# A wait on GpSimd in the attention turns, and the written order of the weight loads behind them, in an attention and spectral feed-forward kernel

## The chip, the cores and the metric

The kernel runs on one core of one Trainium2 chip, as one launch. The metric is device time in microseconds (us). Three runs of the kernel before gave 726.14, 727.07 and 729.10 us; their median is 727.07 us.

## The reference

The inputs are q, k and v of 4 batches, 8 heads, 576 positions and 64 columns, a small network (w1, b1, w2) for a position bias, and two feed-forward weights of float64 numbers. Cut to what matters:

```python
scores = scale * q @ k.T + bias            # bias from relu(x @ w1 + b1) @ w2, x = log distances
attn = exp(scores - max) / (sum + 1e-9)
x = (attn @ v), heads side by side         # (4, 576, 512)
mixed = real(fft(fft(x, axis=1), axis=2))
u = x + mixed
un = (u - mean) / sqrt(var + 1e-06)
out = u + relu(un @ w_ch1) @ w_ch2         # w_ch1 (512, 2048), w_ch2 (2048, 512)
```

## The kernel before, in words

The work has three stages. First the bias is made and the scores of the first unit are begun. Then come the attention turns: a unit is two heads of one batch, there are 16 units, and turn n (`turn_of`, line 552) runs the scores of unit n, the rest of unit n - 1 (transposes, product with v, division) and the preparation of unit n + 1. Turns 1 to 14 are written out as a list of steps (`SECOND`, `ORDER`), the end of the attention as another (`TAIL`). Last come the Fourier products and the feed-forward layers, batch after batch; the first batch is called the first dense batch here (`dense`, called with n_first = 2).

Products are made of float32 numbers split into a high and a low part. In a turn GpSimd makes the splits of unit n + 1 (`prep`, line 203): the steps K1 and K2 for k, L2 and M2 for the second half of q, L1 and M1 for the first half. The M steps are the low parts (line 218), the last of a turn is M1.

The feed-forward weights arrive as float64 words. In ten of the turns (`WIDE`: 2, 3, 5, 6, 7, 9, 10, 11, 13, 14) two blocks are turned into float32, one of the first weight matrix (steps W0 to W3) and one of the second (U0 to U3), by `widen` (line 155). Step 0 is GpSimd's (line 163), steps 1 to 3 are VectorE's (DVE): line 166 clears bits of the raw words, line 167 joins two words, line 168 joins the result to that of step 0. The steps s and t then store a block to memory, f and g load the raw words of the block for the next turn (line 159), y loads v (line 201), k and q load the operands of the unit after next. All these loads and stores go through the queue of SyncE (SP), in the order of the list.

In the turns the order on TensorE (PE), DVE and ScalarE (ACT) is the list's, and from turn 2 on that on GpSimd (POOL) and SP as well. In the list the DVE steps of a turn's second half stand as U1, U2, U3, W1, D8, D7, W2, Y2, Y1, W3, and then D2, D1 of the next turn; a D step adds the bias and takes the row's extreme (line 296), an X step is ACT's exponential (line 311), O copies the product with v out of PSUM (line 501), Y divides into x (lines 526 and 530), P transposes (line 443). z sends two columns of 64 reciprocals across partitions by DMA (`across_halves`, line 514).

Around the first dense batch the order on PE, ACT and GpSimd is still written until `fixed.close()`; that on SP is not, and a scheduler chooses it there. `begin` (the function `first` of `widen_rest`) starts loading the raw words of the six remaining blocks of either matrix, whose widening (`res`) is spread over the batch, with step 0 on ACT (line 161).

Of the kernel before, what the change touches and what calls it, by code (L numbers as in the profile page):

```python
# [9 lines left out]
F32 = mybir.dt.float32  # L10
F32R = mybir.dt.float32r
I32 = mybir.dt.int32
# [8 lines left out]
P = 128  # L21
# [5 lines left out]
L0, L1, L2 = 0, 42, 64  # L27
# [20 lines left out]

ORDER = """
S2 U0 D2 Q0' S1 P0' D1 V0' P2' K1 V2' S4 Q1' S0 K2 D4 D0 P1' S6 L2 M2 P3' D6 S3 V1' P4' V3' W0 V4' S5 R' VR0' D3  # L50
D5 S8 E'' X0 X5 vR1' z' X2 k q U1 U2 S7 A0' X1 U3 W1 D8 L1 X6 D7 A1' A2' X8 X3 W2 t g X4 A3' Y2'' Y1'' A4' O' W3
X7 s y f M1
""".split()

SECOND = """
# [76 lines left out]
def body(ctx, tc, a, out):  # L132
    nc = tc.nc
# [21 lines left out]
    def widen(src, dst, raw, q=nc.sync, on_act=False):  # L155
        words = raw.bitcast(I32).rearrange("p (n t) -> p n t", t=2)
        lo, hi = words[:, :, 0], words[:, :, 1]
        m = dst.bitcast(I32)
        q.dma_start(raw, src)
        if on_act:  # L160
            first = lambda: nc.scalar.activation(dst, hi.bitcast(F32), AF.Copy, scale=2.0 ** -112)
        else:
            first = lambda: nc.gpsimd.tensor_scalar(dst, hi.bitcast(F32), 2.0 ** -112, 0.0, ALU.mult, ALU.add)
        return [
            first,
            lambda: nc.vector.tensor_scalar(hi, hi, -0x80000000, None, ALU.bitwise_and),
            lambda: nc.vector.scalar_tensor_tensor(hi, lo, 29, hi, ALU.logical_shift_right, ALU.bitwise_or),
            lambda: nc.vector.scalar_tensor_tensor(m, m, 3, hi, ALU.logical_shift_left, ALU.bitwise_or),
        ]
# [249 lines left out]
    with ExitStack() as st:  # L419
# [93 lines left out]

        def across_halves(u):
            for h, mine in enumerate(half):
                nc.sync.dma_start(rrs[u][half[1 - h], h:h + 1], rss[u][mine, 8:9])

        def scaled(u, w):
            hp, b = units[u]
# [32 lines left out]
        def turn_of(n, pieces):  # L552

            for i, w in enumerate(SECOND if n == 1 else ORDER):
                w, u = w.rstrip("'"), n - w.count("'")
                if w[0] in "WUstfg":
                    if n >= 2:
                        widened(n, w)
                elif w in PREP:
                    if pieces:  # L560
                        pieces[PREP.index(w)]()
                elif w in "kq":
                    if 2 <= n < U - 2:
                        load(n + 2, [w + "T"])
                elif w == "y":
                    if 1 <= n < U - 1:
                        load_v(n + 1)
                elif 0 <= u < U and (u or n == 1 or w[0] not in "SDX"):
                    steps[w[0]](u, w)
# [7 lines left out]
        wide = {}  # L577

        def raw_tile(rp):
            return rp.tile([P, DM], I64, tag="raw", name="raw")  # L580

        def fetch(which, n):

            f = wide.get("next" + which, 0)
            if f == len(WIDE):
                return
            wide["next" + which] = f + 1
            rp = rawp if which == "W" else rawu
            dst = rp.tile([P, DM], F32, tag="wf", name="wf")
            src, to = (a["m1"][f], w1_d[f].rearrange("p k c -> p (k c)")) if which == "W" else (a["m2"][P * f:P * f + P], w2_d[f])  # L590
            wide[which] = widen(src, dst, raw_tile(rp)) + [lambda: nc.sync.dma_start(to, dst)]

        def widened(n, name):

            if name in "fg":
                if n in WIDE and n + 1 in WIDE:
                    fetch("WU"["fg".index(name)], n + 1)
            elif n in WIDE:
                if name in "st":
                    wide["WU"["st".index(name)]][4]()  # L600
                else:
                    wide[name[0]][int(name[1])]()
# [369 lines left out]
        def dense(ut, tiles, store, n_first=0, mix=None, begin=None):  # L972
# [10 lines left out]
            def w2_load(f):  # L983
                wfs[f] = w2p.tile([P, DM], F32, tag="w2f", name="w2f")
                nc.sync.dma_start(wfs[f], w2_d[f])
# [46 lines left out]
                    store(t)  # L1032

            if n_first:
                for f in range(1, len(WIDE)):
                    w1_load(f)
                    if f < 3:
                        w2_load(f - 1)
                    if f == 3:
                        begin()  # L1040
                w1_load(0)
                part = lambda i: mix.fold(nc.vector, 0, i)
                for step, i in (
                        (w1_parts, 1), (part, 0), (part, 1), (relu_parts, 0), (w2_parts, 0), (part, 2),
                        (mix.fold_hi, 0), (w1_parts, 2), (up, 1), (mix.fold_lo, 0), (relu_parts, 1), (w2_parts, 1),
                        (down, 0)):
                    step(i)
                fixed.close()
            pieces = []
            for f in range(n_first, NF):  # L1050
# [7 lines left out]
        def widen_rest():  # L1058

            token_tile("raw")  # L1060
            raws = [raw_tile(rawp), raw_tile(rawd)] + [
                toks["raw"][:, 1024 * i:1024 * i + 1024].bitcast(I64) for i in range(2)]
            todo = {}

            def start(h):
                f = h // 2
                raw = raws[h % 4]
                if h % 2:
                    dst = (rawp, rawd)[f % 2].tile([P, DM], F32, tag="wf", name="wf")
                    todo[h] = widen(a["m2"][P * f:P * f + P], dst, raw, on_act=True)  # L1070
                    todo[h].append(lambda: nc.sync.dma_start(w2_d[f], dst))
                else:
                    dst = w1[f]
                    todo[h] = widen(a["m1"][f], dst, raw, on_act=True)
                    todo[h].append(lambda: nc.sync.dma_start(w1_d[f].rearrange("p k c -> p (k c)"), dst))

            def first():
                for h in range(2 * len(WIDE), 2 * len(WIDE) + 4):
                    start(h)

            res = []
            for h in range(2 * len(WIDE), 2 * NF):
                early = .1 if h < 2 * len(WIDE) + 2 else 1.
                for c, i in ((.7, 0), (.7, 1), (.8, 2), (.9, 3)):
                    res.append((c * early, lambda h=h, i=i: todo[h][i]()))
                res.append((.05, lambda h=h: todo[h][4]()))
                if h + 4 < 2 * NF:
                    res.append((.05, lambda h=h: start(h + 4)))
            return first, res
# [38 lines left out]
        class Pair:  # L1128
# [119 lines left out]
            def w2_load(self, f, more=False):  # L1248
                rp, tg = (rawd if f % 4 else rawp, "wf") if more and f % 2 == 0 else (w2p, "w2f")
                wf = self.wfs[f] = rp.tile([P, DM], F32, tag=tg, name="w2f")  # L1250
                nc.sync.dma_start(wf, w2_d[f])
# [281 lines left out]
```

## Time and profile before

| | |
|---|---|
| median of three runs | 727.07 us |
| the profiled execution | 727.17 us, of which the span is 725.4 us |
| PE busy | 695.9 us (96%) |
| DVE busy | 477.7 us (66%) |
| ACT busy | 434.6 us (60%) |
| GpSimd busy | 328.6 us (45%) |
| granted clock of PE, mean over the span | 0.993 |

The span is the time from the first to the last instruction of the program. The shares are means over stages with different limits: in the attention turns all four engines are loaded, in the dense batches PE alone is. A time on the left of a row is counted from the span's start. The bracket at a row's end says how long the engine had been idle and what ended it.

### The profile page before, as it was taken

To read this page: it belongs to the slowest core of one execution; us is meant where nothing else is said; L and a number is where in the kernel's file an instruction comes from. 1 tells how busy PE (TensorE), PEld (TensorE's weight loads), DVE (VectorE), ACT (ScalarE), POOL (GpSimd) and SP (SyncE) were. 2 spreads that over 40 slices of the span, in tenths; PEclk is the share of its full clock that TensorE was granted. 3 is DMA by queue.
4 is the path that set the end of the run, shared out by engine and by line. 5 is a ranking of instruction groups with operands and counts; after the bars stand their busy time and mean duration, and the time that the engine had idled before them with its cause. 6 is when DMAs were issued, how large, how long until landed. Compare 5 with 4: busy or idle time off the path is not lost.

```text
span 725.4 us, 15300 instructions
## 1 busy us (share of the span) xinstructions
PE 695.9 (96%) x5787; PEld 559.2 (77%) x5787; DVE 477.7 (66%) x1014; ACT 434.6 (60%) x853; POOL 328.6 (45%) x292
## 2 busy tenths in 40 slices
PE   6999999999999989799999999999999999999997
PEld 3457778778778777588888888878788888888896
DVE  7988697997997977676583766566643434453443
ACT  8998999899989787543433433264434232344453
POOL 0002547447447461344544354568645543444342
PEclk9999999999999999899999999999999999999999
DMA  8887487687687621754421311113222214642432
GB/s 225 213 225 198 155 291 222 182 292 221 195 284 220 229 89 52 275 177 157 147 88 58 102 35 67 35 42 101 100 76 87 73 59 130 212 129 81 131 103 72
DMA packets 49945, 105.72 MB, mean 146 GB/s; under 512 B 8944, under 2 KB 9584, under 8 KB 48752
## 3 DMA queue, kind: packets, MB, share of 16 engines
q1 hardware_dynamic: 49152, 101.09, 45.3%
q0 software_dynamic: 288, 3.08, 1.2%
q8 instruction: 45, 0.74, 0.4%
q10 hardware_dynamic: 432, 0.59, 0.2%
q14 instruction: 28, 0.23, 0.1%
HBM read 81.00 MB, written 21.07 MB: 141 GB/s over the span
## 4 chain that ended last, share of the span: by engine, by line
PE 77%; DMA 6%; ACT 6%; DVE 4%; issue 3%; POOL 2%; SPq 1%; DVEq 0%; POOLq 0%; ACTq 0%
PE hp L998 15%; PE acc L1023 15%; PE acc L1269 12%; PE s L275 6%; PE t L492 6%; PE t L443 4%; PE bps L405 4%; PE hpy L1238 3%; PE hpx L1238 3%; PE hpa L1238 3%; PE zp L705 3%; DMA raw<-m 2%; PE abp L725 2%; ACT p L311 2%; PE hpb L1238 1%
## 5 line engine op out<-in xcount | busy, mean ns | idle before, releaser
L964 POOL TENSOR_TENSOR w2l<-w2f,w2h 128x512 fp32r<-128x512 f32 x64 | 85.2, 1331 | 99.3 <-ACT w2h L963 92.0
L296 DVE CUSTOM_DVE_ANT_0 p<-s,bias 128x576 f32<-128x576 f32 x128 | 93.7, 757 | 27.5 <-PE s L275 23.1
L964 POOL TENSOR_TENSOR w1l<-w,w1h 128x512 fp32r<-128x512 f32 x55 | 72.4, 1317 | 76.5 <-ACT w1h L963 72.5
L311 ACT ACTIVATE p<-p,nm 128x576 f32<-128x576 f32 x128 | 97.7, 765 | 11.9 <-DVE nm L296 11.8
L433 ACT ACTIVATE pt<-t 128x1024 f32<-128x1024 f32 (+2 forms) x97 | 79.1, 868 | 5.5 <-PE t L443 3.4
L492 PE MATMUL t<-pt,v 128*64 128x288 f32 x640 | 81.1, 408 | 0.5 <-ACT pt L433 0.5
L963 ACT ACTIVATE w2h<-w2f 128x512 fp32r<-128x512 f32 x80 | 50.2, 628 | 51.6 <-PE acc L1023 22.2
L1007 DVE SCALAR_TENSOR_TENSOR hl<-hp,hh 128x512 fp32r<-128x512 f32 (+1 forms) x48 | 28.9, 602 | 76.7 <-ACT hh L1006 76.6
L963 ACT ACTIVATE w1h<-w 128x512 fp32r<-128x512 f32 x55 | 34.7, 632 | 65.1 <-PE hp L998 52.3
L492 PEld LDWEIGHTS t<-pt,v 128*64 128x64 f32 x640 | 51.0, 137 | 25.4 <-issue 2.4
L1023 PE MATMUL acc<-w2h,hh 128*128 128x512 f32 x160 | 63.2, 396 | 0.0
L275 PE MATMUL s<-kh,qh 64*128 64x288 f32 (+1 forms) x320 | 59.3, 365 | 3.7 <-DVE nm L296 3.2
L1023 PE MATMUL acc<-w2l,hh 128*128 128x512 f32 x160 | 62.4, 391 | 0.0
L1023 PE MATMUL acc<-w2h,hl 128*128 128x512 f32 x160 | 60.0, 393 | 0.0
L405 PE MATMUL bps<-hd,sm 128*32 128x288 f32 x432 | 50.2, 422 | 8.7 <-DVE hd L385 5.3
L443 PE MATMUL t<-ident,p 64*128 64x64 f32 x1152 | 49.5, 226 | 5.9 <-DVE x L526 2.7
L998 PE MATMUL hp<-uh,w1h 128*128 128x512 f32 x124 | 50.0, 403 | 4.2 <-ACT w1h L963 4.2
L443 PEld LDWEIGHTS t<-ident,p 64*128 64x128 f32 x1152 | 45.7, 141 | 9.5 <-issue 3.9
L214 POOL TENSOR_SCALAR kh<-kT 128x640 fp32r<-128x640 f32 x14 | 10.2, 725 | 90.2 <-PE s L275 74.9
L1269 PE MATMUL acc<-w2h,hh 128*128 128x512 f32 x128 | 50.2, 392 | 0.0
L1269 PE MATMUL acc<-w2h,hl 128*128 128x512 f32 x128 | 50.0, 390 | 0.0
L1269 PE MATMUL acc<-w2l,hh 128*128 128x512 f32 x128 | 49.9, 390 | 0.0
(193 smaller groups left out, 1759.8 us busy)
## 6 DMA issues: line engine op xcount, KB each, us to landing
w2f<-w_d SPq DMA_DIRECT2D x80, 256.0 KB, 2.6
raw<-m SPq DMA_DIRECT2D x32, 512.0 KB, 4.4
w<-w_d SPq DMA_DIRECT2D x43, 256.0 KB, 3.1
qT<-qT SPq DMA_DIRECT2D x32, 288.0 KB, 5.2
bias_d<-ring SPq DMA_DIRECT2D x54, 144.0 KB, 2.6
bias<-bias_d SPq DMA_DIRECT2D x24, 288.0 KB, 4.8
w_d<-wf SPq DMA_DIRECT2D x26, 256.0 KB, 2.5
kT<-kT SPq DMA_DIRECT2D x16, 320.0 KB, 4.9
```

Source lines behind the costliest of these rows:

```text
L275: nc.tensor.matmul(ps[:m, c, :CH], st[e, c0:c0 + m], mv[e, k0:k0 + CH], start=i == 0, stop=i == 2, skip_group_check=True)
L296: nc.vector.tensor_tensor_reduce(p, bank.pop((n, i))[:, :, :CH], bias, -0.125, 3.0e38, ALU.add, ALU.min, nms[n][:, blk:blk + 1])
L311: nc.scalar.activation(p, p, AF.Exp, bias=nms[n][:, blk:blk + 1], scale=-1.0, accum_out=sums[n][:, blk:blk + 1])
L405: nc.tensor.matmul(ps[32 * t4:32 * t4 + 32, c, :CH], w2[:, int(rev)], h[:, c * CH:(c + 1) * CH], start=True, stop=True, tile_position=(0, ...
L433: nc.scalar.activation(dst, src, AF.Copy)
L443: nc.tensor.transpose(tp[:m, e, c0:c0 + 64], src[r], ident[r, r])
L492: nc.tensor.matmul(os_[u][e, c, :CH], vt[u][:, j, e], pts[u][:, 2 * j + h if j < 4 else 8, c * CH:(c + 1) * CH], start=j == 0, stop=j == 4 ...
L963: nc.scalar.activation(h, src, AF.Copy)
L964: eng.tensor_tensor(l, src, h.bitcast(F32), ALU.subtract)
L998: nc.tensor.matmul(ps[:, :N], w[wi][:, P * kb:P * kb + P], ut[ui][:, kb, :N], start=i == 0, stop=i == len(mm) - 1)
L1023: nc.tensor.matmul(acc[t], h[i][:, P * t:P * t + P], w[j], start=f == 0 and k == 0, stop=f == NF - 1 and k == 2)
L1269: nc.tensor.matmul(self.acc[t], h[i][:, P * t:P * t + P], w[j], start=f == 0 and k == 0, stop=f == NF - 1 and k == 2)
```

## The change

The step h is new: a copy of one element by GpSimd that reads the raw words of the first matrix' block after W1 has rewritten them; it stands in the list between L1 and M1, so that M1 (the last step on GpSimd in a turn) comes behind it. M1 had stood at the list's end, and on GpSimd was directly behind L1 there too. The steps y and f change places. For the last unit, `across_halves` issues its two DMAs from ACT's queue instead of SP's. In the first dense batch the order on SP is now written as well: the float32 weight blocks first, in a new order, `begin` behind them. The factor that drew the first two blocks' widening to the front of the batch is gone.

```diff
--- before.py
+++ after.py
@@ -48,8 +48,8 @@
 
 ORDER = """
...
-X7 s y f M1
+D5 S8 E'' X0 X5 vR1' z' X2 k q U1 U2 S7 A0' X1 U3 W1 D8 L1 h M1 X6 D7 A1' A2' X8 X3 W2 t g X4 A3' Y2'' Y1'' A4' O' W3
+X7 s f y
 """.split()
 
 SECOND = """
@@ -513,7 +513,8 @@
 
         def across_halves(u):
             for h, mine in enumerate(half):
-                nc.sync.dma_start(rrs[u][half[1 - h], h:h + 1], rss[u][mine, 8:9])
+                q = nc.scalar if u == U - 1 else nc.sync
+                q.dma_start(rrs[u][half[1 - h], h:h + 1], rss[u][mine, 8:9])
 
         def scaled(u, w):
             hp, b = units[u]
@@ -553,7 +554,7 @@
 
             for i, w in enumerate(SECOND if n == 1 else ORDER):
                 w, u = w.rstrip("'"), n - w.count("'")
-                if w[0] in "WUstfg":
+                if w[0] in "WUstfgh":
                     if n >= 2:
                         widened(n, w)
                 elif w in PREP:
@@ -588,7 +589,10 @@
             rp = rawp if which == "W" else rawu
             dst = rp.tile([P, DM], F32, tag="wf", name="wf")
             src, to = (a["m1"][f], w1_d[f].rearrange("p k c -> p (k c)")) if which == "W" else (a["m2"][P * f:P * f + P], w2_d[f])
-            wide[which] = widen(src, dst, raw_tile(rp)) + [lambda: nc.sync.dma_start(to, dst)]
+            raw = raw_tile(rp)
+            if which == "W":
+                wide["raw"] = raw.bitcast(I32)
+            wide[which] = widen(src, dst, raw) + [lambda: nc.sync.dma_start(to, dst)]
 
         def widened(n, name):
 
@@ -596,7 +600,10 @@
                 if n in WIDE and n + 1 in WIDE:
                     fetch("WU"["fg".index(name)], n + 1)
             elif n in WIDE:
-                if name in "st":
+                if name == "h":
+                    hold = smp.tile([P, 1], F32, tag="hold", name="hold", bufs=1)
+                    nc.gpsimd.tensor_copy(hold[0:1], wide["raw"][0:1, 1:2].bitcast(F32))
+                elif name in "st":
                     wide["WU"["st".index(name)]][4]()
                 else:
                     wide[name[0]][int(name[1])]()
@@ -1032,12 +1039,12 @@
                     store(t)
 
             if n_first:
+                loads = st.enter_context(ExitStack())
+                loads.enter_context(tc.manual_schedule(engines={SP_}))
                 for f in range(1, len(WIDE)):
                     w1_load(f)
-                    if f < 3:
-                        w2_load(f - 1)
-                    if f == 3:
-                        begin()
+                    if f in (1, 4):
+                        w2_load(f // 4)
                 w1_load(0)
                 part = lambda i: mix.fold(nc.vector, 0, i)
                 for step, i in (
@@ -1045,6 +1052,8 @@
                         (mix.fold_hi, 0), (w1_parts, 2), (up, 1), (mix.fold_lo, 0), (relu_parts, 1), (w2_parts, 1),
                         (down, 0)):
                     step(i)
+                begin()
+                loads.close()
                 fixed.close()
             pieces = []
             for f in range(n_first, NF):
@@ -1080,9 +1089,8 @@
 
             res = []
             for h in range(2 * len(WIDE), 2 * NF):
-                early = .1 if h < 2 * len(WIDE) + 2 else 1.
                 for c, i in ((.7, 0), (.7, 1), (.8, 2), (.9, 3)):
-                    res.append((c * early, lambda h=h, i=i: todo[h][i]()))
+                    res.append((c, lambda h=h, i=i: todo[h][i]()))
                 res.append((.05, lambda h=h: todo[h][4]()))
                 if h + 4 < 2 * NF:
                     res.append((.05, lambda h=h: start(h + 4)))
```

GpSimd in turn 13, with the last preparation in the list's order; `hold` is the tile of the new copy, `ql` in the row behind it is M1, and `fs` the Fourier table that is loaded behind turn 13. Before:

```order
97 L218 TENSOR_TENSOR kl<-kT,kh 128x640
98 L214 TENSOR_SCALAR qh<-qT 128x576
99 L218 TENSOR_TENSOR ql<-qT,qh 128x576
100 L163 TENSOR_SCALAR wf<-raw 128x512
101 L214 TENSOR_SCALAR qh<-qT 128x576
102 L218 TENSOR_TENSOR ql<-qT,qh 128x576
103 L617 DMA fs<-fs 128x3840
104 L163 TENSOR_SCALAR wf<-raw 128x512
```

The same place now:

```order
106 L214 TENSOR_SCALAR qh<-qT 128x576
107 L218 TENSOR_TENSOR ql<-qT,qh 128x576
108 L163 TENSOR_SCALAR wf<-raw 128x512
109 L214 TENSOR_SCALAR qh<-qT 128x576
110 L605 COPY hold<-raw 1x1
111 L218 TENSOR_TENSOR ql<-qT,qh 128x576
112 L624 DMA fs<-fs 128x3840
113 L163 TENSOR_SCALAR wf<-raw 128x512
```

The copy stands ahead of M1 and of the table's DMA, and both are behind its wait.

SP between the attention and the first dense batch: `raw` are the words of the remaining blocks, `w_` and `w2f` float32 blocks of the two matrices, `rr` the reciprocals (those of the last unit are the second `rr` row of before). Before:

```order
131 L896 DMA w_5003<-w_d 128x512
132 L516 DMA rr<-rs 64x1 x2
133 L159 DMA raw<-m 128x512
134 L516 DMA rr<-rs 64x1 x2
135 L159 DMA raw<-m 128x512 x2
136 L958 DMA w_5388<-w_d 128x512
137 L985 DMA w2f<-w_d 128x512
138 L958 DMA w_5389<-w_d 128x512
139 L985 DMA w2f<-w_d 128x512
140 L958 DMA w_5389<-w_d 128x512
141 L159 DMA raw<-m 128x512
142 L958 DMA w_5390<-w_d 128x512 x2
```

Now:

```order
131 L903 DMA w_5023<-w_d 128x512
132 L517 DMA rr<-rs 64x1 x2
133 L965 DMA w_5408<-w_d 128x512
134 L992 DMA w2f<-w_d 128x512
135 L965 DMA w_5409<-w_d 128x512 x2
136 L965 DMA w_5410<-w_d 128x512
137 L992 DMA w2f<-w_d 128x512
138 L965 DMA w_5410<-w_d 128x512
139 L965 DMA w_5411<-w_d 128x512 x2
140 L965 DMA w_5412<-w_d 128x512 x2
141 L965 DMA w_5408<-w_d 128x512
142 L159 DMA raw<-m 128x512 x4
```

The first block's load no longer stands behind the last unit's reciprocals and three loads of raw words; the four raw loads come behind all twelve blocks.

ACT at the same place, where `uh` and `w1h` are high parts. Before:

```order
216 L835 ACTIVATE uh<-ut 128x4x128 x4
217 L161 ACTIVATE w_5393<-raw 128x512 x2
218 L161 ACTIVATE wf<-raw 128x512
219 L963 ACTIVATE w1h<-w_5388 128x512
220 L1006 ACTIVATE hh<-hp 128x512
221 L963 ACTIVATE w2h<-w2f 128x512
```

Now:

```order
216 L842 ACTIVATE uh<-ut 128x4x128 x4
217 L517 DMA rr<-rs 64x1 x2
218 L970 ACTIVATE w1h<-w_5408 128x512
219 L1013 ACTIVATE hh<-hp 128x512
220 L970 ACTIVATE w2h<-w2f 128x512
```

The three widening steps ahead of the first `w1h` are gone from there, and two DMAs stand in their place.

## Rows read from the trace of the kernel before

**Rows 1.** Timeline of ACT: the copies at line 501 (start, duration).

```profile
80.67 0.65 ACT L501 ACTIVATE ot<-t 128x576 f32<-128x576 f32 x1 [0.36 <-PE t L492]
...
160.89 0.63 ACT L501 ACTIVATE ot<-t 128x576 f32<-128x576 f32 x1
...
173.40 0.63 ACT L501 ACTIVATE ot<-t 128x576 f32<-128x576 f32 x1
...
240.66 0.63 ACT L501 ACTIVATE ot<-t 128x576 f32<-128x576 f32 x1
...
256.45 0.63 ACT L501 ACTIVATE ot<-t 128x576 f32<-128x576 f32 x1
```

**Rows 2.** Groups of DVE, 88 to 256 us: count | busy us, mean ns | idle before.

```profile
L167 DVE SCALAR_TENSOR_TENSOR raw<-raw 128x512 int32<-128x512 int32 x20 | 17.6, 881 | 0.3
L168 DVE SCALAR_TENSOR_TENSOR wf<-wf,raw 128x512 int32<-128x512 int32 x19 | 16.7, 880 | 0.3
L166 DVE TENSOR_SCALAR raw<-raw 128x512 int32<-128x512 int32 x20 | 13.3, 665 | 0.9 <-POOL wf L163 0.6
```

**Rows 3.** Timelines of DVE and PE around the end of turn 9.

```profile
182.42 0.47 DVE L166 TENSOR_SCALAR raw<-raw 128x512 int32<-128x512 int32 x1
...
184.28 0.69 DVE L167 SCALAR_TENSOR_TENSOR raw<-raw 128x512 int32<-128x512 int32 x1
...
187.07 0.75 DVE L296 CUSTOM_DVE_ANT_0 p<-s,bias 128x576 f32<-128x576 f32 x1
...
188.04 0.30 PE L275 MATMUL s<-kh,qh 64*128 64x288 f32 x2
```

**Rows 4.** Timelines of GpSimd and DVE: the first and the last collision with M1.

```profile
100.87 1.59 POOL L218 TENSOR_TENSOR ql<-qT,qh 128x576 fp32r<-128x576 f32 x1
...
101.24 1.80 DVE L167 SCALAR_TENSOR_TENSOR raw<-raw 128x512 int32<-128x512 int32 x1
...
234.00 1.42 POOL L218 TENSOR_TENSOR ql<-qT,qh 128x576 fp32r<-128x576 f32 x1
...
234.40 1.33 DVE L166 TENSOR_SCALAR raw<-raw 128x512 int32<-128x512 int32 x1
```

**Rows 5.** GpSimd, SP; then a stretch: us, engines' busy times, granted clock, DMA, GB/s.

```profile
235.37 0.73 POOL L617 DMA_DIRECT2D fs<-fs  x1
...
237.59 0.53 SPq L159 DMA_DIRECT2D raw<-m  x1
...
245.67 0.66 POOL L163 TENSOR_SCALAR wf<-raw 128x512 f32<-128x512 f32 x1 [9.56 <-DMA raw<-m]
...
257.90:261.30 3.40, 3.40 (x44) 3.38 (x46) 1.02 (x4) 1.60 (x2) 3.32 (x4) 0.50 0.52 153
```

**Rows 6.** SP, ACT, PE at the dense start; then a stretch there.

```profile
291.76 1.10 SPq L516 DMA_DIRECT2D rr<-rs  x2
...
293.50 0.69 ACT L161 ACTIVATE w<-raw 128x512 f32<-128x512 f32 x1
296.88 0.66 ACT L161 ACTIVATE w<-raw 128x512 f32<-128x512 f32 x1 [2.70 <-DMA raw<-m]
299.56 0.66 ACT L161 ACTIVATE wf<-raw 128x512 f32<-128x512 f32 x1 [2.02 <-DMA raw<-m]
...
300.90 0.80 PE L998 MATMUL hp<-uh,w1h 128*128 128x512 f32 x1 [4.15 <-ACT w1h L963]
...
298.90:305.70 6.80, 4.66 (x10) 3.27 (x11) 4.20 (x4) 3.75 (x7) 4.39 (x3) 0.50 1.03 384
```

**Rows 7.** Timelines of SP (end of turn 5) and GpSimd (turn 6).

```profile
133.85 1.60 SPq L201 DMA_DIRECT2D v<-v  x1
...
140.01 0.70 POOL L163 TENSOR_SCALAR wf<-raw 128x512 f32<-128x512 f32 x1 [1.16 <-DMA raw<-m]
```

**Rows 8.** Landing of the reciprocals' DMAs: 90 to 256 us, then 290 to 300 us.

```profile
DMA to landing us min/median/max: 1.6/5.0/9.5
...
DMA to landing us min/median/max: 1.6/1.7/1.7
```

More of the change, by code (lines that the diff above doesn't have):

```diff
@@ L50 @@
 S2 U0 D2 Q0' S1 P0' D1 V0' P2' K1 V2' S4 Q1' S0 K2 D4 D0 P1' S6 L2 M2 P3' D6 S3 V1' P4' V3' W0 V4' S5 R' VR0' D3
-D5 S8 E'' X0 X5 vR1' z' X2 k q U1 U2 S7 A0' X1 U3 W1 D8 L1 X6 D7 A1' A2' X8 X3 W2 t g X4 A3' Y2'' Y1'' A4' O' W3
-X7 s y f M1
+D5 S8 E'' X0 X5 vR1' z' X2 k q U1 U2 S7 A0' X1 U3 W1 D8 L1 h M1 X6 D7 A1' A2' X8 X3 W2 t g X4 A3' Y2'' Y1'' A4' O' W3
+X7 s f y
 """.split()
```

## The prediction

> **What bounds the kernel now.** I read the busy shares first (the table above), then the chain that ended last, then the timelines of the engines turn by turn. PE is busy for 96% of the span, so time can come only from the few places where it idles, runs at the lower clock, or where a turn is longer than PE's own work. The copy O of line 501 marks the turns: it starts at 80.67 us in turn 1 and at 256.45 in turn 14 [rows 1]. These 13 turns take 175.8 us. Turn 8, which widens nothing, takes 173.40 - 160.89 = 12.51 us; 13 such turns are 162.6. So 13.2 us are lost, nearly all in turns that widen.
>
> The reader is to see why in lines 166 to 168. Their 59 instances sum to 47.6 us [rows 2]. Free ones take 0.47 and 0.69 us [rows 3], so that 20 x 0.47 + 39 x 0.69 = 36.3 are due: 11.3 us too many. The long ones begin while GpSimd is in a split and end about 0.58 us after it: line 167 starts at 101.24, M1 ends at 102.46, line 167 at 103.04 [rows 4]. So DVE waits there until GpSimd's instruction ends. U1, U2, U3 and W1 stand ahead of D8 and D7, whose results ACT needs for the last exponentials ahead of O; a delay there is a delay of the turn. Seven turns (3, 5, 6, 7, 10, 11, 13) have such a collision with M1, of 1.80 - 0.69 = 1.11 us in the first and 1.33 - 0.47 = 0.86 in the last [rows 4]; the seven sum to 7.1.
>
> Two more losses lie behind the turns' row. In turn 14 U0 waits for its raw words until 245.67, 8.1 us after their issue, since the Fourier table is in flight from 235.37 on; that turn takes 256.45 - 240.66 = 15.79 us [rows 1], 3.3 over 12.51, and then PE works from 257.9 to 261.3 at a granted clock of 0.50, the 1.2 GHz level, after idling in pieces [rows 5]. And at the start of the first dense batch PE idles 4.15 us until 300.90, behind ACT, which stood at two widening steps waiting for raw words (2.70 and 2.02 us) with the first high part behind them; the clock is at 0.50 from 298.9 to 305.7 [rows 6].
>
> **The change part by part.** The sum is made against the profiled execution, 727.17 us (span 725.4, 1.8 around it); the median, 727.07, is 0.1 less.
>
> *The hold.* M1 now starts behind W1, so none of U1 to W1 can meet it: 7.1 us go. What comes late next is W2, which stands 184.28 - 182.89 = 1.39 us behind W1's end [rows 3]. M1 takes 1.42 us in the last row of GpSimd there [rows 4], so if it starts h after W1's end, W2 loses about h + 1.42 - 1.39 - 0.11 = h - 0.08 (DVE ends 0.58 after the split instead of 0.69 after its own start, hence the 0.11). This delay is less harmful than the old one, because D8 and D7 are done by then. W2's delay runs through Y, W3, D2 and D1 to the score matmul that needs D1's bank: D1 ends at 187.82 and that matmul starts at 188.04 in turn 9, which has no collision [rows 3]. So 0.2 us are free, and PE loses h - 0.28. The copy is not in the trace. From below it is free and h is 0, and PE loses nothing; from above the copy costs a whole 128x512 step, 0.70 us [rows 7], with some 0.2 for two hand-overs h is 0.9, and PE loses 0.6. I take 0.4, nearer to the small end because the copy moves one element, and 0.12 us in each of ten turns: 1.2 us. Behind the hold on GpSimd stand M1, in turn 13 the table's DMA, and the next turn's U0. U0 waits for its DMA anyway. M1 is needed by the next turn's second score step, some 1.8 us ahead of the 188.04 above, so near 186.2; the new end of M1 is 182.9 + 0.4 + 1.4 = 184.7. That cover of 1.5 us hides M1's move; without it each us too much is one of PE.
>
> The Trainium skill (GPSIMD Engine Reference, Instruction dispatch) says that an instruction's completion does not hold back the next one on GpSimd, since each of its cores goes on by itself. By that rule M1 waits for the hold's semaphore and not for the copy, h is about the two hand-overs, and the 1.2 us are 0; no run here shows it.
>
> *Raw words ahead of v.* At the end of turn 5 the load of v holds SP's queue for 1.60 us, and in turn 6 W0 then waits 1.16 us for its words [rows 7]; W0 and L1 meet U1 and U2 there, for 0.8 us by the same count. Moved ahead, the words come 1.6 us earlier and both steps are through: 0.8 us. In the other turns I count nothing. v itself goes a load later and is used only two turns on.
>
> *Turn 14.* The table's DMA now stands behind the hold and M1, so it starts about 234.4 + 2.3 (U1 to W1 free) + 0.4 + 1.4 = 238.5 instead of 235.4 [rows 5], and the raw words of U0, issued at 237.59 before and 0.9 earlier now, go ahead of it. They need not share the engines with it; I estimate half the 8.1 us, so that U0 starts near 240.8 instead of 245.67. GpSimd then reaches W0 and L1 close to U1, or later if their words share the engines with the table. I leave 1.2 of the 3.3 us and count 2.1. If the table still gets in front, the gain is 0; if all fits, 3.2. The 3.4 us at half clock do 1.7 us of work; with the idle pieces gone I count 1.5.
>
> *The dense start.* The last unit's reciprocals held SP until they went at 291.76 [rows 6], and raw loads followed ahead of the first block's. Now that load waits only for the last product with v (PE, near 291.0). ACT's three widening steps are gone from the front; its two DMAs there take some 0.55 each on SP (1.10 for two), so the first high part starts near 293.5 + 1.1 = 294.6, its low part is done on GpSimd near 296.7, and PE's matmuls before it end at 296.75 (300.90 - 4.15). The idle 4.15 goes. So does the half clock: the 4.66 us that PE works in that stretch [rows 6] are 2.3 at 2.4 GHz, 2.3 us less. Together 6.5. What is late next is the fold of the first Fourier product on DVE, which needs x and so the reciprocals. These are issued 2.4 us later, about 294.2, and landed in 1.7 us on an empty queue, 5.0 in the middle under load [rows 8]. With 1.7 DVE goes on near 296.4, the fold's low part is six steps and, I estimate, 4 to 5 us later, and PE needs it near 300.3 (two dozen matmuls behind 296.75): up to 1.1 us of waiting. With 5.0 it is up to 4.4 and perhaps the half clock again. I take 1.5, nearer to the empty queue since ACT's queue holds nothing else, and count 5.0 (bounds 6.5 and 0).
>
> The Trainium skill (DMA: Bandwidth & Descriptors, Queues, rings and completion order) has each DMA engine go round its queues packet by packet. By it the reciprocals on ACT's queue pass the blocks on SP's, and the 1.5 us would be at most 1.1; if they stood behind the blocks, it would be 4.4. In this trace they shared SP's queue with everything, so it shows only the two ends.
>
> *The later widening* moves ACT and DVE work inside a batch where PE is the bound; its cover is PE's lead, and I count 0 (a rival below takes it away).
>
> Sum: 7.1 - 1.2 + 0.8 + 2.1 + 1.5 + 5.0 = 15.3 us; 727.17 - 15.3 = 711.9 us.
>
> **Rivals.** (a) The collision only changes its place. If the hold wakes late, M1 starts as W2 does, W2 loses the whole of M1 in all ten turns, also in 2 and 9 that have none today: between 0.6 and 1.2 us each. At 0.9 that is 9.0 instead of 1.2: 719.7 us. For it: M1 is longer than the gap to W2. Against it: D8 and D7 cover 1.39 of its 1.42 us.
> (b) The reciprocals land late behind the weight blocks on the same DMA engines: PE waits 4.4 us for the fold and falls to half clock for part of it. The dense start is worth 1.4 instead of 5.0: 715.5 us. For it: the median of 5.0. Against it: a queue of their own.
> (c) The hold does not do what it says: turns are bound by ACT and PE together, and the time DVE wins is spent waiting for scores. Then only the dense start counts: 727.2 - 5.0 = 722.2. For it: turn 8 has little slack either. Against it: turns exceed 12.51 by what their collisions sum to, turn by turn.
> (d) Slower: ACT takes its widening steps in order, and now all raw words are loaded behind twelve blocks. If ACT waits at each for 2.7 us, the longest wait at the dense start [rows 6], and the high part behind it is late for PE, each costs 2.7. Six of the twelve blocks eat the gain up; with eight it is 711.9 + 21.6 = 733.5 us. For it: the same order of things cost 4.15 us before. Against it: by then ACT is a whole layer ahead of PE, some 5 us.
>
> **How the numbers follow.** Forecast 0.56 (its own range 707 to 716), (a) 0.15, (b) 0.13, (c) 0.10, (d) 0.06. The low end takes the hold as free, all of turn 14, no wait for the fold, and 1 us from other steps of GpSimd that no longer meet U1 and U2: 711.9 - 1.2 - 1.3 - 1.5 - 1.0 = 706.9, say 707. The upper end reaches to (a) and into (c): 721. A measurement of this kernel can tell about 0.5%, 3.6 us, from no change. Faster than 723.5: the forecast, (b), nearly all of (a) and half or more of (c), 0.87; within 0.5%: 0.07; slower: 0.06.
>
> **What would show it.** In the profile after: lines 166 to 168 at 0.4 to 0.7 us in U1 to W1, and a W2 of 0.7 to 1.1; M1 starting 0.3 to 0.5 us behind W1's end; O to O near 12.6 us in turns 3, 5, 6, 7 and 13; turn 14's U0 some 5 us earlier against turn 13's M1, and no half clock behind it; at the dense start no PE wait over 1.5 us and the first block's load right behind the last product with v. I am wrong if W2 takes over 1.3 us, if O to O stays at 13.5 us with DVE waiting for PE, or if PE waits in the dense batch for a high part behind a widening step.

## The result, and the profile after

The changed kernel takes 718.09 us (median of 4 runs, 716.2 to 718.73); the kernel before took 727.21 us in the same comparison. The ratio is 0.9862, 95% interval 0.9837 to 0.9887. So 9.1 us were won, where 15.3 were forecast: the direction and the whole range (707 to 721) held; the forecast time, 711.9, did not, and the result lies outside the range that the prediction gave the forecast alone (707 to 716).

Where they came from is read from the copies O, as before [rows 1]. ACT's timeline of the changed kernel, the copies of turns 1, 7, 8, 13, 14 and of the last unit:

```profile
81.23 0.65 ACT L501 ACTIVATE ot<-t 128x576 f32<-128x576 f32 x1 [0.36 <-PE t L492]
...
158.08 0.63 ACT L501 ACTIVATE ot<-t 128x576 f32<-128x576 f32 x1
171.62 0.65 ACT L501 ACTIVATE ot<-t 128x576 f32<-128x576 f32 x1 [0.84 <-PE t L492]
...
235.82 0.63 ACT L501 ACTIVATE ot<-t 128x576 f32<-128x576 f32 x1
250.92 0.63 ACT L501 ACTIVATE ot<-t 128x576 f32<-128x576 f32 x1
...
285.27 0.65 ACT L501 ACTIVATE ot<-t 128x576 f32<-128x576 f32 x1 [1.69 <-PE t L492]
```

| stretch | before, us | after, us | won | forecast |
|---|---|---|---|---|
| to the first O | 80.67 | 81.23 | -0.6 | 0 |
| turns 2 to 13 | 159.99 | 154.59 | 5.4 | 6.7 |
| turn 14 | 15.79 | 15.10 | 0.7 | 2.1 |
| to the last O | 34.54 | 34.35 | 0.2 | 1.5 |
| from the last O on | 434.4 | 431.4 | 3.0 | 5.0 |
| span | 725.4 | 716.7 | 8.7 | 15.3 |

(Before, the last O stands at 290.99; the profiled execution after took 718.73 us.) The turns paid 1.3 us less than forecast, of which turn 8 alone took 1.0 (below). Turn 14 and what follows it paid 0.9 of 3.6, the dense start 3.0 of 5.0.

**The turns.** DVE's groups of lines 166 to 168 in the changed kernel, 88 to 252 us; they answer to [rows 2]:

```profile
L167 DVE SCALAR_TENSOR_TENSOR raw<-raw 128x512 int32<-128x512 int32 x20 | 15.9, 796 | 0.3
L168 DVE SCALAR_TENSOR_TENSOR wf<-wf,raw 128x512 int32<-128x512 int32 x20 | 13.8, 690 | 0.3
L166 DVE TENSOR_SCALAR raw<-raw 128x512 int32<-128x512 int32 x20 | 10.1, 503 | 2.3 <-POOL wf L163 2.0
```

They sum to 39.8 us in 60 instances, where 47.6 in 59 stood before. Line 168 is free in all of its 20. Around the end of turn 9, timelines of DVE and GpSimd, with W1, W2 and then the hold and M1 (compare [rows 3]):

```profile
180.89 0.42 DVE L166 TENSOR_SCALAR raw<-raw 128x512 int32<-128x512 int32 x1
...
182.71 0.78 DVE L167 SCALAR_TENSOR_TENSOR raw<-raw 128x512 int32<-128x512 int32 x1
...
181.38 0.17 POOL L605 COPY hold<-raw 1x1 f32<-1x1 f32 x1 [4.49 <-DVE raw L166]
181.52 1.41 POOL L218 TENSOR_TENSOR ql<-qT,qh 128x576 fp32r<-128x576 f32 x1
```

W1 ends at 181.31, M1 starts at 181.52: h is 0.21 us. W2 takes 0.78 instead of 0.69 us. What is left of collisions is that of W0 and L1 with U1 and U2, where W0's words come late (turn 10, GpSimd and DVE):

```profile
191.18 0.65 POOL L163 TENSOR_SCALAR wf<-raw 128x512 f32<-128x512 f32 x1
191.80 0.87 POOL L214 TENSOR_SCALAR qh<-qT 128x576 fp32r<-128x576 f32 x1
...
192.19 1.03 DVE L167 SCALAR_TENSOR_TENSOR raw<-raw 128x512 int32<-128x512 int32 x1
```

Turns 6, 7, 10 and 11 are 12.9 to 13.1 us for that reason, turns 3, 4, 5, 12 and 13 12.6 to 12.7. Turn 9 is 12.9 without a collision in it; that is not explained.

**Turn 14.** Timelines of DVE, GpSimd and SP in the changed kernel, then a stretch behind the turn (us, the engines' busy times, granted clock, DMA share, GB/s); compare [rows 5]:

```profile
230.36 0.49 DVE L166 TENSOR_SCALAR raw<-raw 128x512 int32<-128x512 int32 x1
...
234.27 0.74 POOL L624 DMA_DIRECT2D fs<-fs  x1
237.35 0.65 POOL L163 TENSOR_SCALAR wf<-raw 128x512 f32<-128x512 f32 x1 [2.35 <-DMA raw<-m]
...
246.21 0.66 POOL L163 TENSOR_SCALAR wf<-raw 128x512 f32<-128x512 f32 x1 [3.71 <-DMA raw<-m]
...
236.72 0.39 SPq L159 DMA_DIRECT2D raw<-m  x1
...
246.91 0.88 DVE L166 TENSOR_SCALAR raw<-raw 128x512 int32<-128x512 int32 x1 [1.98 <-POOL wf L163]
...
251.90:255.40 3.50, 3.04 (x42) 3.03 (x44) 1.57 (x6) 1.64 (x4) 3.50 (x3) 0.51 0.56 173
```

U1 of turn 13 starts at 230.36, and U0 of turn 14 at 237.35, 6.99 us behind it; before it was 245.67 - 234.40 = 11.27 us [rows 4, 5]. But the next raw words, W0's, are issued at 236.72 while the table is in flight, and W0 starts at 246.21. DVE then stands 1.98 us at W1. The wait has gone from one weight's words to the other's, and the half clock behind the turn is still there.

**The dense start.** Timelines of ACT, DVE and PE, then three stretches; compare [rows 6]:

```profile
287.22 0.53 ACTq L517 DMA_DIRECT2D rr<-rs  x1
287.79 0.60 ACTq L517 DMA_DIRECT2D rr<-rs  x1
...
292.82 0.29 DVE L531 TENSOR_TENSOR x<-t,rr 128x128 f32<-128x128 f32 x1 [2.77 <-DMA rr<-rs]
...
295.50 0.63 ACT L699 ACTIVATE gh<-ge 128x512 fp32r<-128x512 f32 x1 [3.27 <-DVE ge L694]
...
296.18 1.31 PE L712 MATMUL zp<-fs,gh 128*128 128x320 f32 x4 [2.19 <-ACT gh L699]
...
288.00:291.00 3.00, 3.00 (x13) 2.48 (x14) 2.05 (x4) 0.63 (x1) 1.30 (x1) 1.00 0.89 271
291.00:293.00 2.00, 2.00 (x11) 1.63 (x10) 0.18 (x1) 1.12 (x2) 0.70 (x1) 1.00 0.03 3
...
295.90:299.70 3.80, 3.52 (x13) 3.52 (x14) 2.16 (x5) 2.69 (x6) 2.31 (x2) 0.56 1.01 332
```

The 4.15 us in front of the first `w1h` are gone. The reciprocals, issued at 287.22 and 287.79, land 5.3 and 4.9 us later, when the five blocks issued from 285.31 on are through (the DMA engines are 0.89 busy until 291 and idle then). DVE waits 2.77 us for them. PE waits 2.19 us for the fold, and runs some 3.5 us at about half clock behind it. Part of the 2.19 us is one more collision: the fold's first step on DVE (`pq`) begins beside a split on GpSimd.

```profile
292.30 1.30 POOL L971 TENSOR_TENSOR w2l<-w2f,w2h 128x512 fp32r<-128x512 f32 x1 [1.80 <-ACT w2h L970]
...
293.03 1.66 DVE L692 TENSOR_TENSOR pq<-x 128x1024 f32<-128x1024 f32 x1
```

In experiment 10, where it begins ahead of that split, `pq` takes 1.22 us, so 0.44 us are the split's. In experiment 3 `pq` begins 0.2 us sooner behind the last O, takes 1.88 us, and PE waits the same 2.19.

### The profile page after: what moved, and what is told of

It reads as the page before. It is cut to its first block, busy times and chain, and to the rows that moved or that the text cites. A ratio compares the mean times of both kernels' runs of the same rounds, so it can differ in the third digit from the quotient of the medians.

```text
span 716.7 us, 15317 instructions
## 1 busy us (share of the span) xinstructions
PE 692.2 (97%) x5787; PEld 559.4 (78%) x5787; DVE 469.6 (66%) x1014; ACT 434.8 (61%) x853; POOL 327.6 (46%) x302
## 4 chain that ended last, share of the span: by engine, by line
PE 87%; ACT 4%; DMA 3%; DVE 2%; issue 1%; POOL 1%; SPq 0%; DVEq 0%; ACTq 0%; POOLq 0%
PE acc L1030 15%; PE hp L1005 15%; PE acc L1277 12%; PE t L492 10%; PE s L275 9%; PE t L443 6%; PE bps L405 5%; PE hpy L1246 3%; PE zp L712 3%; PE hpx L1246 3%; PE hpa L1246 3%; PE abp L732 2%; PE hpb L1246 1%; DMA raw<-m 1%; ACT ring L351 1%
```

## The experiments

Each ran in five rounds beside the kernel before (728.1 to 728.4 us there). The gain of one against the changed kernel is worked out from the two ratios to the kernel before, times 728. Each ratio's interval is 1.6 to 2.0 us to either side in experiments 4 to 11, so such a gain is uncertain by some 2.5 us.

**1. The hold alone,** on the kernel before (`L1 h M1` in the list, M1 away from the end, the step h; nothing else).

> The kernel before with the hold alone: step h and M1 behind it; raw words still behind v, the old dense start. Theory (the hold pays the collisions with M1 back in full and costs next to nothing itself): the copies O of turns 2 to 13 lie 160.0 us apart in sum before and 154.6 after the whole change; I expect 154.8 to 155.6 here, line 166 to 168 free of M1 in U1 to W1, the dense start as before (PE idle near 4 us), so 5 to 6 us in all, near 721.5 us. The turn behind the Fourier table gains under 1 us. Rival c of the prediction (turns are bound elsewhere): O to O stays near 13.3 us on average and the time near 727.

722.38 us, ratio 0.9926 (0.9909 to 0.9942): 5.4 us faster. Turns 2 to 13 take 153.7 us in the profile, 6.3 less than before; lines 166 to 168 sum to 39.7 in 59 instances. The dense start is as before (PE waits 4.19 us). So the hold's part stands by itself, and rival (c) falls. Turn 14 was expected to gain up to 1 us; it got 0.84 us longer (16.63). GpSimd there, with the table, U0 and W0:

```profile
231.68 0.74 POOL L623 DMA_DIRECT2D fs<-fs  x1
234.18 0.67 POOL L163 TENSOR_SCALAR wf<-raw 128x512 f32<-128x512 f32 x1 [1.77 <-DMA raw<-m]
...
245.20 0.65 POOL L163 TENSOR_SCALAR wf<-raw 128x512 f32<-128x512 f32 x1 [5.85 <-DMA raw<-m]
```

The hold by itself already moves the wait from U0's words to W0's.

**2. Raw words ahead of v, alone.**

```diff
-X7 s y f M1
+X7 s f y M1
```

> The kernel before with the steps y and f exchanged, and nothing else: raw words ahead of v. The prediction's term: 0.8 us, from turn 6 alone, 726.3 us. Rival: nothing that can be measured (M1 still collides, and a step W0 that comes earlier only meets other steps), 727.1 plus or minus 1. Where it is worth more, step W0 must wait under 1 us for its words in turns 5, 6 and 10 and lines 166 to 168 must sum to less than 47.6 us.

727.98 us, ratio 1.0002 (0.9987 to 1.0017): nothing. In the profile (span 724.5) turns 5, 6 and 13 are 0.5, 0.75 and 0.8 us shorter, turns 7 and 14 0.55 and 0.8 longer; the three lines sum to 45.9 us in 60 instances. What one turn wins is partly lost in another.

**3. The dense part alone,** on the kernel before (ACT's queue for the last reciprocals, SP's written order, `begin` behind it, no early factor).

> The kernel before with the dense part alone (the last unit's reciprocals from ACT's queue, SP's written order, raw words last, no early factor). From the trace after: the idle time and half clock at the dense start fall from about 7 us to about 4, so 3 us, 724.2 us; PE then waits some 2 us for the fold's high part and is at half clock for 3 to 4 us behind it. The prediction's term was 5.0 (722.2). The reciprocals should land about 5 us after their issue here too, if it is the blocks ahead of them that hold them.

724.92 us, ratio 0.9957 (0.9938 to 0.9977): 3.1 us faster. PE waits 2.19 us for the fold's high part, the reciprocals land after 4.2 and 4.7 us, and what follows the last O takes 431.8 us, near the changed kernel's 431.4. The order on SP, `begin`'s place and the dropped factor were not tried apart from each other. The parts sum to 5.4 + 0 + 3.1 = 8.5 us; the whole change has 8.7 by the spans, 9.1 by the medians and 10.0 by its ratio.

**4. The changed kernel without the hold.**

```diff
-... U3 W1 D8 L1 h M1 X6 D7 ...
+... U3 W1 D8 L1 M1 X6 D7 ...
```

> The changed kernel with the step h taken out and M1 right behind L1 again. If the hold is worth 5.5 to 6.5 us and the parts add, this is 718.1 + 6 = 724 us, with the collisions of M1 back in lines 166 to 168 in seven turns and O to O near 13.5 us there. If the earlier raw words carry part of it, it is nearer to 721.

724.22 us, ratio 0.9949 (0.9929 to 0.9969): 6.3 us slower than with it. Turns 3, 5, 6, 7, 10 and 11 are back at 13.6 to 14.2 us, but turns 2 to 13 together are only 4.3 us longer than in the changed kernel (158.85 us; 5.2 if the changed kernel's unexplained wait of 0.94 us in turn 8, below, is set aside). Another 3.0 us are turn 14, which takes 18.11 us. GpSimd and SP there:

```profile
233.24 0.73 POOL L624 DMA_DIRECT2D fs<-fs  x1
...
236.36 1.35 SPq L159 DMA_DIRECT2D raw<-m  x1
...
247.06 0.66 POOL L163 TENSOR_SCALAR wf<-raw 128x512 f32<-128x512 f32 x1 [13.10 <-DMA raw<-m]
```

Without the hold the table goes 3.1 us ahead of U0's words, with it 1.5 us behind them (234.27 against 232.75). So the totals, 5.4 alone and 6.3 here, agree, but they are made up of different parts: part of the hold's worth in the changed kernel is the later issue of the table.

**5. The Fourier table a turn earlier.**

```diff
-            if n == U - 2:
+            if n == U - 3:
                 fs = tabp.tile(...)
```

> The changed kernel with the Fourier table's DMA issued one turn earlier, ahead of turn 13 instead of ahead of turn 14. Theory (turn 14 stays long because the raw words, this time those of W0, share the DMA engines with the table: they were issued at 236.72 us and W0 could start at 246.21): turn 14 falls from 15.1 to 12.7 us, W0 there waits under 1 us, the idle pieces and the half clock behind it go, 1.5 to 3 us more, so 4 to 5 us in all, near 713.5 us. Rival 1: the table only meets the operands of turn 13, that turn gets longer by what turn 14 loses, 718 us. Rival 2: the half clock behind turn 14 comes from the end of the attention itself, and only 2.4 us are won, 715.7 us.

715.57 us, ratio 0.982 (0.9795 to 0.9845): 3.1 us faster than the changed kernel, less than the theory had and little more than the uncertainty. The profiled execution is the slowest of its five (717.78), its span only 0.7 us below the changed kernel's; so the trace does not show where all of the 3.1 us come from. Turn 14 is 14.36 (0.7 less) and the stretch behind it loses its half clock (1.3 less), but turn 13 is 13.90 (1.2 more): GpSimd waits there for kT, and its later steps meet U1 to U3. Two of its rows, GpSimd and DVE in turn 13:

```profile
225.43 0.73 POOL L214 TENSOR_SCALAR kh<-kT 128x640 fp32r<-128x640 f32 x1 [0.75 <-DMA kT<-kT]
...
231.16 1.08 DVE L167 SCALAR_TENSOR_TENSOR raw<-raw 128x512 int32<-128x512 int32 x1
```

Rival 1 holds in part: the table takes its price wherever something else is being loaded.

**6. The last reciprocals back on SP's queue.**

```diff
-                q = nc.scalar if u == U - 1 else nc.sync
+                q = nc.sync
                 q.dma_start(...)
```

> The changed kernel with the last unit's reciprocals back on SP's queue, ahead of the first block's load; nothing else differs. In the changed kernel they were issued at 287.2 and 287.8 us behind five blocks (1.3 MB) issued from 285.31 on, and landed 5.1 us later; the fold waited 2.77 us for them and PE 2.19 us for the fold. Theory (they land late because the blocks are ahead of them in the DMA engines, whatever the queue): on SP they go at 286.1 with nothing ahead, land by 289, the fold is 3 us earlier and PE's 2.19 us and most of the half clock go; the first block comes 1.9 us later, which costs PE about 1 us at its low part. 1.5 to 3 us faster, 715 to 716.5 us. Rival (a DMA of 64 pieces of 4 bytes takes 5 us by itself there): they land at 291, the fold gains 1 us, the first block loses 1: 718 us.

715.41 us, ratio 0.9831 (0.9806 to 0.9857): 2.3 us faster than from ACT's queue, which the times alone do not show clear of the noise; in the trace what follows the last O is 1.9 us shorter (429.6). The reciprocals go first and land after 1.6 and 1.7 us; PE does not wait for the fold and stays at full clock there. It waits 0.42 and 1.12 us for the first block's parts instead, as expected.

**7. Fewer blocks ahead of the reciprocals,** still on ACT's queue.

```diff
                     w1_load(f)
-                    if f in (1, 4):
-                        w2_load(f // 4)
+                    if f == 1:
+                        w2_load(0)
+                        w2_load(1)
```

> The changed kernel with the second block of the second matrix loaded right behind the first one. Its room is free only when the division with the reciprocals is done, and so the three blocks behind it in SP's order wait too: the reciprocals, still on ACT's queue, have two blocks (0.5 MB) ahead of them instead of five. If the bytes ahead decide, they land in 2.5 to 3.5 us instead of 5.1, the fold is 2 us earlier, PE waits under 0.5 us for it and stays at full clock or nearly: 2 to 3.5 us faster, 715 to 716 us. If ACT's queue is slow by itself they take 5 us as before, and it is 718 us. The order of later work in the first dense batch differs from that of the changed kernel; the dense start is read from the trace.

715.56 us, ratio 0.9835 (0.9813 to 0.9857): 2.0 us faster, within the noise by the times; in the trace what follows the last O is 2.5 us shorter (428.9). In its trace the DMA issues from 285 to 295 us, and a stretch:

```profile
rr<-rs ACTq DMA_DIRECT2D x2, 0.2 KB, 2.7
...
292.00:296.00 4.00, 3.92 (x22) 3.32 (x21) 3.03 (x5) 2.10 (x5) 2.24 (x2) 1.00 0.95 306
```

The reciprocals land after 2.9 and 2.5 us, PE has no wait over 0.4 us at the dense start, and the clock stays at 1.00. With none, two and five blocks ahead (6, 7 and the changed kernel) the reciprocals take 1.7, 2.7 and 5.1 us: on ACT's queue the landing goes with the blocks ahead on SP's, and a queue of their own does not take them past.

**8. The hold fourfold.**

```diff
-                    nc.gpsimd.tensor_copy(hold[0:1], wide["raw"][0:1, 1:2].bitcast(F32))
+                    for _ in range(4):
+                        nc.gpsimd.tensor_copy(hold[0:1], wide["raw"][0:1, 1:2].bitcast(F32))
```

> The changed kernel with the hold's copy made four times. One took 0.17 us, so M1 starts 0.72 instead of 0.21 us behind W1. By the prediction's formula W2 loses 0.5 us more in each of ten turns (0.78 becomes 1.3 us) and PE h - 0.28 = 0.44 us: 4.4 us, 722.5 us. Rival (D8 and D7, done by then, leave room for it, and only W2, Y and D2 move): O to O stays at 12.65 us in the turns without other collisions, 718 to 719 us.

720.7 us, ratio 0.9912 (0.9892 to 0.9932): 3.6 us slower. GpSimd and DVE in turn 9:

```profile
183.44 0.88 POOL L606 COPY hold<-raw 1x1 f32<-1x1 f32 x4 [4.29 <-DVE raw L166]
184.29 1.40 POOL L218 TENSOR_TENSOR ql<-qT,qh 128x576 fp32r<-128x576 f32 x1
...
182.94 0.44 DVE L166 TENSOR_SCALAR raw<-raw 128x512 int32<-128x512 int32 x1
184.77 1.48 DVE L167 SCALAR_TENSOR_TENSOR raw<-raw 128x512 int32<-128x512 int32 x1
```

Four copies took 0.88 and not 0.68 us, so h is 184.29 - 183.38 = 0.91. W2 takes 1.48; the formula gives 0.69 + 0.91 - 0.08 = 1.52. PE's part by the formula is 0.91 - 0.28 = 0.63 in a turn behind one that widens. Turns 3, 4 and 12, which in both kernels have no collision but W2's, got 0.61, 0.67 and 0.70 longer: the formula holds, with its 0.2 us of room. Turns 6, 7, 10 and 11 got only 0.28 to 0.40 longer; there U1 and U2 meet fewer of W0 and L1 than in the changed kernel (none in turns 6 and 10). Turn 5 got 0.27 longer and turn 9 0.26 shorter, which the formula does not explain. Turns 2 to 13 got 3.05 longer in all; the changed kernel's unexplained wait in turn 8 (0.94 us), which is missing here, hides part of the price.

**9. The Fourier table behind the last M1 of turn 14.**

```diff
-            if n == U - 2:
-                fs = tabp.tile(...)
-                nc.gpsimd.dma_start(fs, a["fs"])
             turn_of(n, pr)
+            if n == U - 2:
+                fs = tabp.tile(...)
+                nc.gpsimd.dma_start(fs, a["fs"])
```

> The changed kernel with the Fourier table's DMA issued behind the last M1 of turn 14 instead of ahead of that turn. One turn earlier it only moved the trouble: turn 14 fell by 0.7 us and turn 13 rose by 1.2, since the table then met kT and qT there. Here no raw words and no operands are left to load in turn 14's wake, and the first product with the table is 15 us away. Theory (turn 14's 2.5 us over 12.6 and part of what follows are the price of the table in flight): W0 of turn 14 waits under 1 us, turn 14 is 12.6 to 13.2 us, turn 13 stays at 12.7, PE idles 2 us less behind it; 3 to 4.5 us faster than the changed kernel, 713.5 to 715 us. Rival (the half clock and the idle pieces behind turn 14 belong to the end of the attention): only the 2 us of turn 14, 716 us.

712.78 us, ratio 0.9792 (0.9767 to 0.9816): 5.1 us faster than the changed kernel. GpSimd in turn 14, and two stretches:

```profile
236.72 0.65 POOL L163 TENSOR_SCALAR wf<-raw 128x512 f32<-128x512 f32 x1 [2.90 <-DMA raw<-m]
...
241.83 0.66 POOL L163 TENSOR_SCALAR wf<-raw 128x512 f32<-128x512 f32 x1
...
246.81 0.74 POOL L625 DMA_DIRECT2D fs<-fs  x1
...
246.80:253.00 6.20, 5.39 (x102) 4.58 (x98) 4.96 (x13) 5.33 (x12) 5.45 (x5) 1.00 0.77 259
289.00:296.00 7.00, 4.80 (x24) 3.75 (x24) 5.09 (x8) 3.10 (x6) 3.21 (x3) 1.00 0.79 260
```

W0 has no wait, turn 14 is 13.04 us, and the turn to the next O 14.76 instead of 16.05: 3.35 us in these two. Against the kernel before, turn 14 and the way to the last O are then 4.2 us shorter (2.75 and 1.48), where the prediction had counted 3.6. Turn 13 is 13.60 us and not 12.7 as expected, since W0 and L1 meet U1 to U3 there; nothing was changed in that turn, and with the table at the same place it is 12.66 in experiment 10. The half clock is gone behind turn 14 and, not expected, at the dense start as well, though PE still waits 2.20 us for the fold there; from the last O on it is 430.2 us, 1.3 less.

**10. Both 9 and 7.**

> The changed kernel with both: the table behind turn 14's M1, and the second block of the second matrix loaded right behind the first (two blocks ahead of the last reciprocals instead of five). The second alone gave 2.5 us. If the two places are independent the gains add, 3.5 + 2.5 = 6 us, near 712 us, which is what the prediction had for the change itself (711.9); then its two missing terms are these two. If one takes the other's gain (both clear one half-clock stretch), 714 us.

711.27 us, ratio 0.9767 (0.9744 to 0.9791): 6.9 us faster than the changed kernel, where 5.1 and 2.0 add to 7.1. This is the lowest median of all, 2.3% under the kernel before, but 1.8 us from experiment 9's, which is within the uncertainty. The traces do not show that the two gains add: from the last O on it is 429.9 us, only 0.2 less than in experiment 9, where the clock stayed up already. Of the 1.9 us between the two spans 1.0 lie in turns 2 to 14 and 0.7 ahead of the first O. PE waits 1.26 us for the fold here (the reciprocals take 1.7 and 3.4 us), and 0.98 of it is the fold's second step on DVE, `ge`, beside GpSimd's split (it takes 0.69 free):

```profile
286.80 1.62 POOL L971 TENSOR_TENSOR w2l<-w2f,w2h 128x512 fp32r<-128x512 f32 x1 [1.77 <-ACT w2h L970]
...
287.30 1.67 DVE L694 TENSOR_TENSOR ge<-pq 128x512 f32<-128x512 f32 x1
```

**11. The hold behind W2.** The step h stands behind W2 in the list, and so reads what W2 has written; the order on every engine stays.

```diff
-... W1 D8 L1 h M1 X6 D7 A1' A2' X8 X3 W2 t g ...
+... W1 D8 L1 X6 D7 A1' A2' X8 X3 W2 h M1 t g ...
```

> The changed kernel with the hold reading the words after W2 instead of after W1, so that M1 starts 2.2 us later; the order on every engine stays. W2 then meets nothing (0.69 instead of 0.78 us), but M1 lies beside Y2, Y1 and W3: from the trace it would run from 183.7 to 185.1 in turn 9, W3 starts at 184.2 and would end 0.8 us late if it waits as lines 166 to 168 do. Theory (what is behind W3 has 0.2 to 0.3 us of room): 0.5 us in each of ten turns, 5 us slower than the changed kernel, 723 us. Rival (D2 and D1 have more room, the delay ends there): 718 us, or 0.9 us less for the free W2.

722.55 us, ratio 0.9923 (0.9896 to 0.9951): 4.4 us slower than the changed kernel, near the theory's 5. W3 (line 168) takes 1.45 to 1.49 instead of 0.68 us in all ten turns that widen, and M1 itself is late for PE in three places (0.39, 0.90 and 2.40 us). Of the three places tried for M1 (behind L1, behind W1, behind W2) only the one behind W1 leaves DVE's steps nearly free.

## Why the prediction was right or wrong

The direction was right, and the largest term for the reason given. That the time fell into the whole range was in part luck: its upper end was drawn for rivals (a) and (c), which did not happen. What used it up were shortfalls at turn 14 and the dense start and a wait in turn 8 that no term had.

*The hold* was right in its mechanism. 7.1 - 1.2 = 5.9 us were forecast and 5.4 measured for it alone (experiment 1; 6.3 in turns 2 to 13 of that trace). In the changed kernel it is worth 6.3 by the times; in the traces 4.3 lie in turns 2 to 13 and 3.0 in turn 14 (experiment 4). h was 0.2 instead of 0.4, W2 took 0.78 where 0.7 to 1.1 was expected. The formula for W2 held up to h = 0.91, and so did its step to PE in the turns without other collisions (experiment 8). At h = 0.21 it gives PE no loss at all, so the 1.2 us were too dear and the small end of the bounds was the right one. M1 starts 0.14 us after the start of a copy of 0.17. That agrees with what the Trainium skill (GPSIMD Engine Reference, Instruction dispatch) says, that a completion does not hold back the next instruction. But a copy is not free: in experiment 8 three more moved M1 by 0.70 us, 0.23 each.

One reading of the rows was too wide. That a long step ends 0.58 us behind GpSimd's split holds for lines 167 and 168 only; line 166 ends 0.31 us behind it (235.73 against 235.42 in [rows 4]), and `pq` 1.09 us (294.69 against 293.60). With free times of 0.43, 0.69 and 1.22 us, each ends its own free time less 0.1 behind the split, as if it did nearly all of its work after it.

*Raw words ahead of v:* 0.8 forecast, 0 within 1.2 either way (experiment 2). Turns 5, 6 and 13 got shorter, turns 7 and 14 longer: "in the other turns I count nothing" was the mistake, since an earlier W0 meets other steps there.

*Turn 14* is the step that failed. "I leave 1.2 of the 3.3 us and count 2.1", and 1.5 for the clock; 0.7 and 0.2 came. The first half was right: U0's words no longer wait for the table, and U0 starts 6.99 us behind turn 13's U1, where the prediction's 240.8 - 234.4 = 6.4 stood. But the words of W0 come next, and the prediction named them ("or later if their words share the engines with the table") without pricing them. From their issue to W0's start it took 9.5 us, and W1 waited. Experiment 9 shows that the 3.6 us were there to be had (4.2 against the kernel before): they come when the table is issued where no load is waited for.

*The dense start* was right in its sign and sized too high: 5.0 forecast, 3.0 (profile) and 3.1 (experiment 3) measured. The idle 4.15 us went as forecast. The term that was off is the landing of the reciprocals: between 1.7 and 5.0 us the prediction leaned to 1.7 "since ACT's queue holds nothing else", and it was 5.1, the condition of rival (b). PE's wait was then 2.19 (1.5 forecast, 4.4 in the rival), and the half clock stayed for 3.5 us. Experiments 6 and 7 show the cause, the blocks ahead; 0.44 of the 2.19 us are GpSimd's split beside `pq`, which the prediction had not looked for. The Trainium skill (DMA: Bandwidth & Descriptors, Queues, rings and completion order) has an engine go round its queues packet by packet, so that a queue of its own would have let the reciprocals pass; here they landed behind all five blocks, and the measurement decides.

*Rivals (a) and (d)* did not happen: W2 lost 0.09 us and not a whole M1, and no widening step in the dense batch held PE. ACT does wait 2.58 and 2.65 us at two of them, at 314.62 and 325.75, but PE has no wait there. Rival (c) fell with experiment 1.

Two losses belong to no step. Turn 8 got 1.0 us longer, from one PE wait for nothing that the profile shows (below), and the first O came 0.6 us later though nothing ahead of it was changed: in the thirteen traces it stands between 79.60 and 82.00.

## What to carry to other kernels

When a wait is taken from one transfer that shares the DMA engines with a long one, ask which transfer is issued next: here it stood where the first one had stood, and of what was tried only a later issue of the long one took the wait away. A small transfer on a queue of its own still landed behind the bytes that were issued before it on another, so count the blocks ahead, not the queues. And a wait put into a list to keep two engines apart costs only what it moves past the next pair that meet: a copy of one element between W1 and M1 started M1 0.2 us behind W1 and gave 5.4 us. A total that comes out as forecast can still be made up of other parts, so compare it stretch by stretch.

## What the runs showed of the hardware that was not expected

One instruction of PE in turn 8 waits for nothing that the profile names. In the changed kernel's PE timeline:

```profile
165.20 0.29 PE L275 MATMUL s<-kh,qh 64*128 64x288 f32 x1 [0.94 <-issue]
```

The same matmul waits 1.46 us in experiment 3, 0.49 in 6 and 0.74 in 7, and not in the other traces, that of before among them. All four have the changed dense part; six others have it too, without the wait. What it is stays open.

The half clock does not follow from one wait alone. In the changed kernel and in experiments 3, 4, 5, 8 and 11 PE waits 2.19 us for the fold at the dense start, and the granted clock falls to 0.50 for 3 to 4 us. In experiment 9 it waits 2.20 us and the clock stays at 1.00. What else differs there is that the clock had not fallen behind turn 14; but in experiment 5 it had not either. The runs do not settle it.
